# A pointwise convolution with folded depthwise weights on one core: splitting the weight load, moving the first input load to ScalarE's queue, and reordering the last waits

## The chip, the core and the metric

The kernel runs on one core of one Trainium2 chip. The metric is the time of one execution on the device in microseconds (us). Every time below that is given from "the start of the span" comes from the profile of one execution. The profiled span is a little shorter than the timed execution: the span of the kernel before is 572.9 us, and the profiled execution itself was timed at 574.59 us.

The engines are called by their short names in the profile: PE is TensorE (its weight loads, which overlap its matmuls, have a row of their own, PEld), DVE is VectorE, ACT is ScalarE, POOL is GpSimd and SP is SyncE. A "q" behind a name (SPq, ACTq) means the engine's sequencer, for instance when it issues a DMA.

## The reference, cut to what matters

A depthwise convolution with a 1x1 window multiplies each channel by one number; a pointwise convolution then mixes the channels with a 384x384 matrix.

```python
H = W = 384; C = 384; k = 1          # x: (1, 384, 384, 384) bf16, dw: (1, 1, 384), pw: (384, 384)
xp = jnp.pad(x, ((0,0),(pad,pad),(pad,pad),(0,0)))         # pad = 0 for k = 1
out = jnp.zeros_like(x)
for i in range(k):
    for j in range(k):
        out = out + xp[:, i:i+H, j:j+W, :] * dw[i, j][None, None, None, :]
return jnp.einsum('bhwc,cd->bhwd', out, pw)
```

With a 1x1 window this is `x @ (diag(dw) @ pw)` for 147,456 pixels. x and the output have 113 MB each.

## The kernel before

The kernel scales `pw` by `dw` once, at the start, and then does one matrix product. The pixels are cut into 288 "supertiles" of 512. Each supertile is transposed by DVE (pairs of bf16 moved as 32-bit words, two instructions for the two halves of the channels), multiplied on PE in 48 matmuls, copied from PSUM to SBUF by ACT, and stored. Loads and stores handle 1 to 10 supertiles at a time ("chunks"); the first chunks have 1, 1, 2, 2 and 4 supertiles, and their loads are called x0 to x4 here. The loads go into three big buffers in rotation.

The start of the program prepares the folded weights `w_r`. Four things play a role there.

The loads, in the order of their issue (SP issues all but `dw`):

```python
nc.scalar.dma_start(dw_row[:], dw.rearrange("a e c -> a (e c)")).then_inc(s_dw, 16)
nc.sync.dma_start(pw_n[:], pw.rearrange("(k p) d -> p k d", p=P)).then_inc(s_pw, 16)
load_x(0)
# ... cut: SP goes on with x1, x2, x3, x4, then the loop of loads and stores
```

The small matmuls on PE. `idle_work(n)` issues 4n matmuls on constants ("fillers") whose result nobody reads; they keep PE occupied. The three matmuls on `dw_row` turn the row of depthwise weights into columns. Then 18 matmuls multiply `pw` by selection matrices `sel_w` that carry the depthwise weights; the table `times` says which of them are repeated for the sake of being busy:

```python
idle_work(4)
nc.tensor.wait_ge(s_dw, 16)
# ... cut: 3 matmuls on dw_row, then_inc(s_df)
idle_work(4)
nc.tensor.wait_ge(s_pw, 16)
times = {(1, 1): 3, (2, 0): 2}
for k in range(3):
    nc.tensor.wait_ge(s_sw, k + 1)
    for r in range(2):
        if k == 2:
            nc.tensor.wait_ge(*w_done[r])      # the PSUM half is free again: copy r is done
        for v in [0, 1] * times.get((k, r), 1):
            mm = nc.tensor.matmul(PS[(k + 1) % 2][:, 2 * r + v, :D],
                lhsT=sel_w[...k, r...], rhs=pw_n[64 * v : 64 * v + 64, k, :], ...)   # cut
        mm.then_inc(s_w)
```

The copies of the six weight parts out of PSUM. Part 1 is copied by DVE, the parts 0, 2, 3, 4 and 5 by ACT, in this order, each as soon as its matmuls are done. The first matmul of the main loop needs parts 0, 1, 2 and 3 and the first half of the first transposed supertile:

```python
w_eng = [1, 0, 1, 1, 1, 1]                                  # 0: DVE, 1: ACT
w_first = {(0, 0): [(0, 1), (1, 3)], (4, 0): [(1, 4)], (4, 1): [(1, 5)]}
```

DVE's own program in this stage is: the selection matrices (`sel`, `dw_f`, three `sel_w`), the copy of part 1, and then the transposes of supertiles 0, 1, 2 and so on, each after its load:

```python
if h == 0 and j == 0:
    nc.vector.wait_ge(sem, n)                               # this chunk's load
ins = nc.vector.transpose(out=Tw[:, 3 * h : 3 * h + 3], in_=Xw[...])     # cut
if jj >= 2:
    ins._wait_ge(s_pe, 2 * (jj - 2) + h + 1)                # the buffer is free again
ins.then_inc(s_t[s][h])
```

At the end, the last supertile is copied by ACT and DVE together, in four pieces, and stored in two parts, and SP waits for the last stores:

```python
if jj + 1 == NS:
    nc.vector.wait_ge(s_o[g % NR], 16 * sum(map(len, groups[g % NR : g : NR])))
    nc.vector.wait_ge(s_pe, 2 * jj + 2)
    nc.scalar.wait_ge(s_pe, 2 * jj + 2)
    for q in (0, 2):
        nc.scalar.copy(Ov[:, q, j, :], PS[s][:, q, :D]).then_inc(s_a[s])
        nc.vector.tensor_copy(Ov[:, q + 1, j, :], PS[s][:, q + 1, :D]).then_inc(s_d)
    continue
```

```python
for o in sorted(range(NR), key=lambda o: (o - len(groups)) % NR):      # the order 2, 0, 1
    n = sum(n_parts[t] for t, c in enumerate(chunks) if c[0] % NR == o)
    nc.sync.wait_ge(s_o[o], 16 * n)
```

Of the kernel before, what the change touches and what calls it, by code (L numbers as in the profile page):

```python
# [13 lines left out]
NR = 3  # L14
# [4 lines left out]
def _groups(n_super: int):  # L19

    head, tail = [[1, 1, 2, 2, 4]], [[6, 4], [4, 2, 1, 1]]
    mid = n_super - sum(map(sum, head + tail))
    assert mid > 0 and mid % LMAX == 0
    return head + [[LMAX]] * (mid // LMAX) + tail
# [3 lines left out]
def kernel(  # L28
# [12 lines left out]
    nc = tc.nc  # L41
    P = nc.NUM_PARTITIONS
    B, H, W, C = x.shape
# [10 lines left out]
    groups = _groups(NS)  # L54
# [14 lines left out]
    pw_n = consts.tile([P, 3, D], BF16, name="pw_n")  # L69
# [19 lines left out]
    s_pe = nc.alloc_semaphore("s_pe")  # L89
# [2 lines left out]
    s_o = [nc.alloc_semaphore(f"s_o{i}") for i in range(NR)]  # L92
    s_dw = nc.alloc_semaphore("s_dw")
    s_pw = nc.alloc_semaphore("s_pw")
    s_df = nc.alloc_semaphore("s_df")
    s_sw = nc.alloc_semaphore("s_sw")
    s_dwf = nc.alloc_semaphore("s_dwf")
# [4 lines left out]
    with tc.tile_critical(sync_engine=mybir.EngineType.Pool, no_gpsimd_drain=True):  # L102
        def x_of(t):
            g, i, off, first, L = chunks[t]
            n = first + LONG - NS
            if n >= 0:
                return Xl[:, 4 * n : 4 * n + 4, :], s_xl[n], 16
            n = sum(len(ls) > i for ls in groups[g % NR : g + 1 : NR])
            return Xs[g % NR][:, 4 * off : 4 * (off + L), :], s_x[g % NR][i], 16 * n

        def load_x(t, eng=nc.sync):
            g, i, off, first, L = chunks[t]
            dst, sem, _ = x_of(t)
            rows = xf[512 * first : 512 * (first + L), :]
            if first + LONG < NS:
                src = rows.rearrange("(p s) c -> p (s c)", p=P)
                dst = dst.rearrange("p s c -> p (s c)")
                if i == 0 and g >= NR:
                    je = g_end[g - NR]
                    eng.wait_ge(s_t[je % 2][1], je // 2 + 1)  # L120
            else:
                src = rows.rearrange("(a k q) c -> q a k c", k=4, q=4)
            eng.dma_start(dst, src).then_inc(sem, 16)
# [22 lines left out]


        nc.scalar.dma_start(dw_row[:], dw.rearrange("a e c -> a (e c)")).then_inc(s_dw, 16)
        nc.sync.dma_start(pw_n[:], pw.rearrange("(k p) d -> p k d", p=P)).then_inc(s_pw, 16)
        load_x(0)  # L150

        todo = []
        for t, (g, i, off, first, L) in enumerate(chunks):
# [4 lines left out]
        for _, f, a in sorted(todo, key=lambda a: a[0]):  # L158
# [4 lines left out]
                for _ in range(28):  # L163
                    nc.sync.wait_ge(s_pw, 16)
            f(*a)
        for o in sorted(range(NR), key=lambda o: (o - len(groups)) % NR):
            n = sum(n_parts[t] for t, c in enumerate(chunks) if c[0] % NR == o)
            nc.sync.wait_ge(s_o[o], 16 * n)

# [37 lines left out]
        def idle_work(n):  # L207
            for _ in range(n):
                for i in range(4):
                    nc.tensor.matmul(  # L210
                        PS[0][:, 2 * (i % 2) + i // 2, :D],
                        lhsT=ones[32 * i : 32 * i + 32, 0:P],
                        rhs=ones[32 * i : 32 * i + 32, :],
                        start=True,
                        stop=True,
                        tile_position=(32 * i, 0),
                    )
# [10 lines left out]
                stop=True,  # L228
            )
        mm.then_inc(s_df)  # L230
        idle_work(4)
        nc.tensor.wait_ge(s_pw, 16)
        times = {(1, 1): 3, (2, 0): 2}
        for k in range(3):
            nc.tensor.wait_ge(s_sw, k + 1)
            for r in range(2):
                if k == 2:
                    nc.tensor.wait_ge(*w_done[r])

                for v in [0, 1] * times.get((k, r), 1):  # L240
                    mm = nc.tensor.matmul(  # L241
                        PS[(k + 1) % 2][:, 2 * r + v, :D],
                        lhsT=sel_w[64 * v : 64 * v + 64, k, r, :, :].rearrange("p q w -> p (q w)"),
                        rhs=pw_n[64 * v : 64 * v + 64, k, :],
                        start=True,
                        stop=True,
                        tile_position=(64 * v, 0),
                    )
                mm.then_inc(s_w)
# [18 lines left out]
        def transposes(t, j):  # L268
            g, i, off, first, L = chunks[t]
            jj = first + j  # L270
            s = jj % 2
            X, sem, n = x_of(t)
            Xw = X.bitcast(U32).rearrange("p (k l) c -> p k l c", l=L)
            Tw = Ts[s][:].bitcast(U32).rearrange("p b (i k) -> p b k i", k=4)
            for h in range(2):
                if h == 0 and j == 0:
                    nc.vector.wait_ge(sem, n)
                ins = nc.vector.transpose(  # L278
                    out=Tw[:, 3 * h : 3 * h + 3],
                    in_=Xw[:, :, j, 96 * h : 96 * h + 96].rearrange("p k (b w) -> p b k w", w=32),  # L280
                )
                if jj >= 2:
                    ins._wait_ge(s_pe, 2 * (jj - 2) + h + 1)
                ins.then_inc(s_t[s][h])
# [29 lines left out]
        for jj, (t, j) in enumerate(order):  # L314
            g, i, off, first, L = chunks[t]
            s = jj % 2
            Ov = Os[g % NR][:, 4 * off * D : 4 * (off + L) * D].rearrange("p (q j d) -> p q j d", q=4, d=D)
            if j == 0 and i == 0 and g >= NR:
                nc.scalar.wait_ge(s_o[g % NR], 16 * sum(map(len, groups[g % NR : g : NR])))
            if jj + 1 == NS:  # L320
                nc.vector.wait_ge(s_o[g % NR], 16 * sum(map(len, groups[g % NR : g : NR])))
                nc.vector.wait_ge(s_pe, 2 * jj + 2)
                nc.scalar.wait_ge(s_pe, 2 * jj + 2)
                for q in (0, 2):
                    nc.scalar.copy(Ov[:, q, j, :], PS[s][:, q, :D]).then_inc(s_a[s])  # L325
                    nc.vector.tensor_copy(Ov[:, q + 1, j, :], PS[s][:, q + 1, :D]).then_inc(s_d)  # L326
                continue
            a = nc.scalar.copy(Ov[:, :, j, :], PS[s][:, :, :D])  # L328
            a._wait_ge(s_pe, 2 * jj + 2)
            a.then_inc(s_a[s])  # L330

            if jj in LONG_AT:
                load_x(NT - LONG + LONG_AT.index(jj), nc.scalar)
            if jj + 2 < NS:
                transposes(*order[jj + 2])
# [30 lines left out]
```

## Time and profile before

| what | value |
|---|---|
| time, median of 3 runs | 574.9 us (574.84 to 575.03) |
| profiled span | 572.9 us |
| busy PE matmul / PEld / DVE / ACT | 566.9 / 412.3 / 508.0 / 418.7 us |
| moved over DMA, mean rate | 226.88 MB, 396 GB/s |
| main-loop matmuls | 13,824, busy 561.8 us |
| first main-loop matmul starts at | 6.76 us |
| landing after issue: pw, x0, x1, x2 | 2.9, 3.3, 5.6, 7.0 us |

The table is read from the start of the page (busy times, DMA), from its list of the costliest groups (the matmuls), from the timeline (the start of the main loop) and from the DMA view with a window on one issue at a time (the landings). 561.8 us of matmuls in 288 supertiles are 1.95 us for each. What lies outside of the main loop is 6.76 us at the start and the few microseconds from the last matmul to the end of the span.

### The profile page before, as it was taken

Reading aid. Unit: us, or ns where it says so; the run is one execution under the profiler, and the core shown is the slowest. Engines: PE = TensorE matmul, PEld = TensorE weight load, DVE = VectorE, ACT = ScalarE, POOL = GpSimd, SP = SyncE. Lnnn points to the kernel's source line nnn. Section 1 sums busy time; section 2 is a strip of 40 time slices with the busy share of each in tenths; the row PEclk is TensorE's granted clock in tenths of the full one; section 3 lists DMA queues with packets and bytes.
Section 4 is the critical chain, followed back from the end, with each engine's and each line's share of the span. In section 5 each row is a group of like instructions: output and inputs, shape, how many; then the busy total and the mean of one; then the engine's idle time right before and its main releaser. Section 6 shows DMA issues by size and latency. Waiting matters only on the chain.

```text
span 572.9 us, 29723 instructions
## 1 busy us (share of the span) xinstructions
PE 566.9 (99%) x13877; PEld 412.3 (72%) x13877; DVE 508.0 (89%) x584; ACT 418.7 (73%) x297; POOL 0.5 (0%) x5
## 2 busy tenths in 40 slices
PE   8999999999999999999999999999999999999996
PEld 5777777777777777777777777777777777777774
DVE  7899999999999999999999999999999999999995
ACT  6777777777777777777777777777777777777775
POOL 0000000000000000000000000000000000000000
PEclk9999999999999999999999999999999999999999
DMA  8999999999999999999999999999999999999676
GB/s 323 435 374 428 424 419 433 433 431 417 431 404 424 390 403 409 418 390 393 437 391 391 400 425 398 389 414 428 398 385 428 405 389 401 422 398 373 262 285 245
DMA packets 26453, 226.88 MB, mean 396 GB/s; under 512 B 1226, under 2 KB 6987, under 8 KB 22603
## 3 DMA queue, kind: packets, MB, share of 16 engines
q1 hardware_dynamic: 25408, 226.01, 97.3%
q10 hardware_dynamic: 1034, 0.79, 0.4%
q14 instruction: 10, 0.07, 0.0%
q8 instruction: 1, 0.02, 0.0%
HBM read 113.54 MB, written 113.25 MB: 396 GB/s over the span
## 4 chain that ended last, share of the span: by engine, by line
PE 98%; ACT 1%; DMA 0%; DVE 0%; issue 0%; DVEq 0%
PE ps L193 97%; PE ps L210 0%; DMA out_dram<-O 0%; ACT w_r L291 0%; ACT O L328 0%; DVE O L326 0%; DVEq L102 0%; PE ps L241 0%; PE ps L223 0%
## 5 line engine op out<-in xcount | busy, mean ns | idle before, releaser
L193 PE MATMUL ps<-w_r,T 32*128 32x384 bf16 x13824 | 561.8, 321 | 0.5 <-ACT w_r L291 0.5
L278 DVE STREAM_TRANSPOSE T<-X 128x384 uint32<-128x384 uint32 x572 | 501.2, 881 | 54.9 <-DMA X<-in_x_dram 2.9
L328 ACT CAST O<-ps 128x1536 bf16<-128x1536 f32 x287 | 412.7, 1438 | 147.3 <-PE ps L193 147.3
L193 PEld LDWEIGHTS ps<-w_r,T 32*128 32x128 bf16 x13824 | 410.0, 93 | 152.3 <-issue 0.9
L291 ACT CAST w_r<-ps 128x768 bf16<-128x768 f32 x5 | 3.6, 820 | 1.3 <-PE ps L241 1.3
L210 PE MATMUL ps<-const-bfloat16-1.0 32*128 32x384 bf16 x32 | 2.8, 517 | 1.1 <-PEq L350 1.1
L278 DVE STREAM_TRANSPOSE T<-Xl 128x384 uint32<-128x384 uint32 x4 | 3.5, 880 | 0.4
L326 DVE CAST O<-ps 128x384 bf16<-128x384 f32 x2 | 1.0, 552 | 3.1 <-DMA out_dram<-O 3.1
L266 ACT ACT_TABLE_LOAD x1 | 1.3, 1283 | 1.5 <-POOLq L102 1.5
L241 PE MATMUL ps<-pw_n,sel_w 64*128 64x384 bf16 x18 | 2.4, 423 | 0.0
L210 PEld LDWEIGHTS ps<-const-bfloat16-1.0 32*128 32x128 bf16 x32 | 1.1, 124 | 1.6 <-issue 1.4
L241 PEld LDWEIGHTS ps<-pw_n,sel_w 64*128 64x128 bf16 x18 | 1.0, 120 | 1.6 <-issue 0.7
L291 DVE CAST w_r<-ps 128x768 bf16<-128x768 f32 x1 | 1.0, 959 | 1.0 <-PE ps L241 1.0
L296 DVE TENSOR_REDUCE sel<-eye 128x64 f32<-128x128 bf16 x1 | 0.3, 289 | 1.5 <-POOL eye L256 1.5
L325 ACT CAST O<-ps 128x384 bf16<-128x384 f32 x2 | 0.9, 482 | 0.5 <-PE ps L193 0.5
L303 DVE COPY dw_f<-ps 128x3 f32<-128x3 f32 x1 | 0.2, 160 | 0.9 <-PE ps L223 0.9
L306 DVE TENSOR_SCALAR sel_w<-sel,dw_f 128x256 bf16<-128x256 f32 x3 | 0.9, 349 | 0.0
L223 PEld LDWEIGHTS ps<-const-bfloat16-1.0,dw_row 1*128 1x128 bf16 x3 | 0.3, 115 | 0.4 <-DMA dw_row<-in_dw_dram 0.4
L256 POOL TENSOR_SCALAR_AFFINE_SELECT eye<-const-bfloat16-1.0 128x128 bf16<-128x128 bf16 x1 | 0.3, 292 | 0.6 <-POOLq L102 0.6
L266 ACT COPY warm<-const-float32-0.0 128x1 f32<-128x1 f32 x2 | 0.3, 188 | 0.0
L223 PE MATMUL ps<-const-bfloat16-1.0,dw_row 1*128 1x1 bf16 x3 | 0.3, 176 | 0.0
L350 POOL MEMSET const-bfloat16-1.0<- 128x1 bf16 x1 | 0.1, 102 | 0.0
(3 smaller groups left out, 0.3 us busy)
## 6 DMA issues: line engine op xcount, KB each, us to landing
X<-in_x_dram SPq DMA_DIRECT2D x26, 3840.0 KB, 21.9
out_dram<-O SPq DMA_DIRECT2D x26, 3840.0 KB, 27.7
X<-in_x_dram SPq DMA_DIRECT2D x3, 1536.0 KB, 17.9
out_dram<-O SPq DMA_DIRECT2D x4, 768.0 KB, 9.3
out_dram<-O SPq DMA_DIRECT2D x2, 1536.0 KB, 15.1
X<-in_x_dram SPq DMA_DIRECT2D x3, 768.0 KB, 8.4
X<-in_x_dram SPq DMA_DIRECT2D x1, 2304.0 KB, 19.6
out_dram<-O SPq DMA_DIRECT2D x1, 2304.0 KB, 11.4
```

Of the source, the lines that this page charges most:

```text
L193: mm = nc.tensor.matmul(PS[s][:, q, :D], lhsT=Ts[s][32 * q : 32 * q + 32, b, par::2], rhs=w_r[32 * q : 32 * q + 32, b, par, :], start=(b, ...
L210: nc.tensor.matmul(PS[0][:, 2 * (i % 2) + i // 2, :D], lhsT=ones[32 * i : 32 * i + 32, 0:P], rhs=ones[32 * i : 32 * i + 32, :], start=True ...
L223: mm = nc.tensor.matmul(PS[1][:, 0, D + k : D + k + 1], lhsT=dw_row[:, P * k : P * k + P], rhs=ones[0:1, 0:1], start=True, stop=True,)
L241: mm = nc.tensor.matmul(PS[(k + 1) % 2][:, 2 * r + v, :D], lhsT=sel_w[64 * v : 64 * v + 64, k, r, :, :].rearrange("p q w -> p (q w)"), rhs ...
L256: nc.gpsimd.affine_select(out=eye[:], in_=ones[:, 0:P], pattern=[[-1, P]], compare_op=mybir.AluOpType.is_equal, fill=0.0, base=0, channel_ ...
L266: nc.scalar.copy(warm[:, s : s + 1], nc.const_aps.tensor(0.0, [P, 1], F32)).then_inc(s_a[s])
L278: ins = nc.vector.transpose(out=Tw[:, 3 * h : 3 * h + 3], in_=Xw[:, :, j, 96 * h : 96 * h + 96].rearrange("p k (b w) -> p b k w", w=32),)
L291: o = nc.vector.tensor_copy(out, in_) if e == 0 else nc.scalar.copy(out, in_)
L306: nc.vector.tensor_scalar_mul(sel_w[:, k], sel[:].unsqueeze(2).to_broadcast([P, 2, 4, 32]), dw_f[:, k : k + 1]).then_inc(s_sw)
L325: nc.scalar.copy(Ov[:, q, j, :], PS[s][:, q, :D]).then_inc(s_a[s])
L326: nc.vector.tensor_copy(Ov[:, q + 1, j, :], PS[s][:, q + 1, :D]).then_inc(s_d)
L328: a = nc.scalar.copy(Ov[:, :, j, :], PS[s][:, :, :D])
```

## The change

The change touches the start and the end of the program; the main loop is the same.

1. `pw`'s first 128 rows, which the first four of the weight matmuls need, are loaded by a DMA of their own with their own semaphore (96 KB); the other 256 rows follow in a second DMA (192 KB). It is meant to let the weight matmuls of `k = 0` begin before all of `pw` is there.
2. The first input load, x0, is issued by ScalarE, so that SP has again as many issues ahead of x1 as before.
3. The second group of fillers shrinks from 16 matmuls to 8, and the repeated weight matmuls move: three rounds for (1, 1) become one, and (2, 1) gets two. The weight stage has 16 matmuls in place of 18.
4. At the end, SP waits for the three store semaphores in the order 1, 0, 2 in place of 2, 0, 1, and DVE waits for PE ahead of the stores in the program text. In the built programs the wait that stands first in the text is the one that ends up on the instruction itself, and the others become semaphore instructions ahead of it. So in the program before, DVE's copy carries the wait for an old store and a separate instruction waits for PE; after the change the copy carries the wait for PE. Likewise SP's closing branch carried the wait for the buffer 2, and carries that for the buffer 1, which is stored last, after the change.

```diff
-        nc.sync.dma_start(pw_n[:], pw.rearrange("(k p) d -> p k d", p=P)).then_inc(s_pw, 16)
-        load_x(0)
+        nc.sync.dma_start(pw_n[:, 0], pw[0:P, :]).then_inc(s_pw, 16)
+        nc.sync.dma_start(pw_n[:, 1:3], pw[P:C, :].rearrange("(k p) d -> p k d", p=P)).then_inc(s_pw2, 16)
+        load_x(0, nc.scalar)
@@ SP's last waits
-        for o in sorted(range(NR), key=lambda o: (o - len(groups)) % NR):
+        for o in sorted(range(NR), key=lambda o: (len(groups) - 1 - o) % NR):
@@ PE's start
-        idle_work(4)
+        idle_work(2)
         nc.tensor.wait_ge(s_pw, 16)
-        times = {(1, 1): 3, (2, 0): 2}
+        times = {(2, 0): 2, (2, 1): 2}
         for k in range(3):
+            if k == 1:
+                nc.tensor.wait_ge(s_pw2, 16)
             nc.tensor.wait_ge(s_sw, k + 1)
@@ the last supertile
             if jj + 1 == NS:
+                nc.vector.wait_ge(s_pe, 2 * jj + 2)
                 nc.vector.wait_ge(s_o[g % NR], 16 * sum(map(len, groups[g % NR : g : NR])))
-                nc.vector.wait_ge(s_pe, 2 * jj + 2)
```

(Cut: the allocation of the semaphore `s_pw2`.)

More of the change, by code (lines that the diff above doesn't have):

```diff
@@ L94 @@
     s_pw = nc.alloc_semaphore("s_pw")
+    s_pw2 = nc.alloc_semaphore("s_pw2")
     s_df = nc.alloc_semaphore("s_df")
```

## The prediction

> **What bounds the kernel now.** I read the chain that ended last first, because a change at the two ends of a program can only be worth what those ends take from it. Its columns are start, length (both us) and what ran.
>
> ```profile
> 0.80 0.32 issue
> 1.12 1.49 PE ps L210 x16
> 2.61 0.03 PE ps L223
> 2.64 1.30 PE ps L210 x13
> 3.94 0.45 PE ps L241 x2
> 4.39 0.02 issue
> 4.41 2.21 ACT w_r L291 x3
> 6.62 0.14 issue
> 6.76 557.91 PE ps L193 x13728
> ```
>
> The last row is the main loop. It never stops: 288 supertiles of 1.95 us are 561.6 us, and 6.76 + 561.6 = 568.4, while the last supertile's copy starts at 568.59. So the time is the start (6.76), the loop (561.6) and what follows (572.9 - 568.4 = 4.5 us). No part of the change touches the middle term. Only the start and the end, 11.3 us together, are in play, and 2% would be 11.5 us.
>
> The chain puts the filler (L210) ahead of the first weight matmul at 3.94. That is not what released it. The timeline of 3.8 to 7.2 us (start, length, engine, line, operation, then the idle time before it and what ended it) says that it was the load of pw:
>
> ```profile
> 3.87 0.13 PEld L241 LDWEIGHTS ps<-pw_n,sel_w 64*128 64x128 bf16 x4 [0.62 <-DMA pw_n<-in_pw_dram]
> ...
> 4.41 3.61 ACT L291 CAST w_r<-ps 128x768 bf16<-128x768 f32 x5 [1.33 <-PE ps L241]
> ...
> 5.61 1.55 DVE L278 STREAM_TRANSPOSE T<-X 128x384 uint32<-128x384 uint32 x2
> ```
>
> So the start is a relay: pw lands at 0.96 + 2.9 = 3.82; PE makes part 0 (3.87 to about 4.4); ACT copies parts 0, 2, 3 (4.41 to 6.62), after which PE starts with 0.14 us of issue. The five copies take 3.61 us, their starts some 0.69 apart. The transposes of x0 start at 5.61 with no idle time before them: x0, landed at 1.45 + 3.3 = 4.8, had been waiting for DVE.
>
> Just behind it stand the next two loads. The same timeline from 7.2 to 11 us:
>
> ```profile
> 7.60 1.58 DVE L278 STREAM_TRANSPOSE T<-X 128x384 uint32<-128x384 uint32 x2 [0.45 <-DMA X<-in_x_dram]
> ```
>
> x1 landed at 1.97 + 5.6 = 7.58. DVE's first half of it takes 0.88 (mean on the page), to 8.48; with the 0.14 us that PE's issue took above, supertile 1 can start at 8.62, and it does start at 6.76 + 1.95 = 8.71. **Slack 0.09 us.** For x2: transposed from 9.56 (idle before it, ended by its DMA), 9.56 + 0.88 + 0.14 = 10.58 against 10.66, slack 0.08. So three things end almost together: the weights, x1 and x2.
>
> The end, in the timeline from 568.5 on:
>
> ```profile
> 568.59 0.86 ACT L325 CAST O<-ps 128x384 bf16<-128x384 f32 x2 [0.51 <-PE ps L193]
> 568.66 1.02 DVE L326 CAST O<-ps 128x384 bf16<-128x384 f32 x2 [3.08 <-DMA out_dram<-O]
> 569.24 0.85 SPq L142 DMA_DIRECT2D out_dram<-O  x2
> ```
>
> ACT and DVE wait for the same last matmul; DVE starts 0.07 later. "DMA out_dram" is named because that wait sits on the copy, but that store was long done.
>
> **What the Trainium skill says.** "DMA: Bandwidth & Descriptors", section "Queues, rings and completion order": SP and ACT each have a ring on each of the same 16 DMA engines, and an engine alternates between rings, but only after draining a whole packet of several descriptors. The trace before fits: a 384 KB load that ACT issues at 24.55 us begins to move only near 28.7 and lands near 43, because SP's ring is full of large transfers. [...] Here pw's last data packet starts at about 3.4 and the load counts as landed at 3.82: some 0.37 us after that packet's end, so splitting a load does not split this part. "TensorE: Matmul & The Clock Gate", Part 1, says that PE runs at half clock until a free-running window of about 3.4 us has been busy. In the trace, groups of weight matmuls start 0.32 us apart until about 5.1 and 0.16 apart from 5.4 on, some 4.3 us after PE's first filler at 1.12.
>
> **The change, part by part.**
>
> *pw's first rows.* The first 128 of pw's 384 packets had moved by about 2.7 us in the packet records; with the 0.37 for the receipt the small load lands near 3.1. The next wait takes over: `sel_w` for k = 0 is written by DVE from 2.87 to about 3.22, and PE has seen it at 3.3. So the first weight matmul starts near 3.37 in place of 3.87, and ACT's first copy near 3.91. With the copies unchanged (2.21 + 0.14) the loop could start at 6.26: **0.50 us at most**. The fillers are no obstacle: 8 of them, from 2.4 in groups of four 0.32 us apart, are through near 3.2.
>
> *pw's other rows.* Parts 2 and 3 need the second load. From its landing f the path is 0.05 + 0.50 (matmul) + 0.04 + 0.69 + 0.82 (two copies) + 0.14 = 2.24. The start is max(6.26, f + 2.24), break-even at f = 4.52. If pw's second part moves ahead of x0 on the engines, as today, f is about 3.85 and nothing is lost. If x0 on the other ring gets in between, its 8 packets of 0.12 us per engine come ahead of up to 16 of pw, about 1 us: f near 4.4 (finely mixed) to 4.8 (x0 first), so the start is 6.64 to 7.04.
>
> *x0 on ScalarE's queue.* SP issues about every 0.49 us. pw takes two slots now, so x1 keeps the third (1.97); x0 is issued by ACT behind dw at about 1.5, as early as before. The same 1.06 MB must move by x1's landing and the same 1.84 MB by x2's. I find nothing that brings x1 or x2 forward. In the packet records a few engines spend 1.0 to 1.8 us on their first packet of x1 (4.1 to 4.3 us) and of x2, which makes them late; nothing in the change addresses that. ACT's table load (1.28) and its two small copies move back by about 0.5, to end near 3.6, still ahead of 3.91.
>
> *Gain at the start, then:* the loop's end follows the latest of the three gates. If x1 and x2 land as before, supertiles 1 and 2 start 0.09 and 0.08 earlier at best, and the other 0.4 us becomes an idle gap of PE between supertiles 0 and 1. **About -0.08 us.**
>
> *The last waits.* DVE's copy starts with ACT's: -0.07 on the path, as its second copy (ends 569.68) releases the last store. SP's closing branch passes one semaphore instruction less after the last landing: in the records that instruction and the branch behind it start at 571.71 and 571.78, so -0.07. **About -0.13 us**, and this is the safest part.
>
> Sum: 574.9 - 0.08 - 0.13 = 574.7.
>
> **The rivals.** (1) *The full half microsecond arrives*: x1 and x2 land earlier as well, because two rings hide those long first packets or because x0 no longer stands ahead of them in SP's ring. Then -0.50 - 0.13 gives 574.3. For it: the DMA rate was only 164 to 292 GB/s between 4.4 and 6.8 us against 410 after that, so there is room. Against: bytes and issue times are the same. (2) *pw's second load becomes the wait*: x0 gets in front, f is 4.8, the loop starts at 7.04, +0.28 - 0.13 gives 575.05. For it: engines alternate between rings, and by 2.6 us some engines are still busy with pw's first rows, so x0 is next. Against: with pw's second part at 1.45 and x0 at about 1.5, pw's descriptors should be first on an idle engine. (3) *The clock*: with 8 fillers and 2 weight matmuls less, PE has more gaps before 5.4. If the switch to full clock slips past the start of the loop by 1 us, that microsecond yields half, +0.5. For it: idle from about 3.9 if f is late. Against: the first copies, not PE, set the pace, and the repeats in k = 2 fill the time from about 4.7 on.
>
> **Range and chances.** Roughly half of the weight goes to the small gain near 574.7, a sixth to rival 1, a third to rivals 2 and 3 with 575.0 to 575.3. The runs before spread over 0.2 us. Range 574.2 to 575.3. 2% is out of reach either way.
>
> **What would show it.** The first weight matmul at 3.3 to 3.5, released by DVE or the load; ACT's first copy near 3.9; the gap between its first and second copy (0.69 if f is early, over 1 us if rival 2 holds); the first L193 matmul at 6.2 to 6.7; a gap in PE before supertile 1 that a transpose of x1 ends; the spacing of weight matmuls for the clock; DVE's last copy level with ACT's. The prediction is wrong if x1 and x2 land half a microsecond or more away from 7.6 and 9.5 us, in either direction, or if the clock switches late.

## The result, and the profile after

| | before | after |
|---|---|---|
| time, median | 575.0 us (6 runs) | 576.84 us (6 runs, 576.24 to 577.43) |
| ratio, 95% interval | | 1.0028 (1.0015 to 1.0041) |
| profiled span | 572.87 us | 575.71 us |
| pw (after: its second part) lands | 3.82 us | 6.37 us |
| x0 lands | 4.78 us | 6.54 us |
| first main-loop matmul | 6.76 us | 8.44 us |
| first supertile on PE | 1.95 us | 3.26 us |
| ACT's first last copy to the end of the span | 4.28 us | 4.14 us |

The changed kernel is slower by 1.8 us, 0.3% of the time. The profiled execution is the slowest of the six (577.43 us), 2.84 us above that of the kernel before, so it shows more loss than the median does. Its account is exact for itself: the loop starts 1.68 us later, the first supertile takes 1.31 more, the end takes 0.14 less. The sum is +2.85; the spans differ by 2.84.

The chain that ended last, after the change (start, length, what):

```profile
1.40 4.98 DMA pw_n<-in_pw_dram
6.37 0.05 issue
6.42 0.35 PE ps L245 x2
6.77 0.02 issue
6.80 1.51 ACT w_r L295 x2
8.30 0.14 issue
8.44 559.21 PE ps L195 x13063
```

Before, this chain named PE's fillers and three copies by ACT. Now one DMA holds 4.98 us of it: the second part of pw, issued at 1.40. Behind it come only two copies, as the copy of part 0 was done long before. The timeline of the same stretch shows the two sides of the split (start, length, engine, line, operation, and the idle time before it):

```profile
3.37 0.82 PE L245 MATMUL ps<-pw_n,sel_w 64*128 64x384 bf16 x4
3.91 0.80 ACT L295 CAST w_r<-ps 128x768 bf16<-128x768 f32 x1 [0.40 <-PE ps L245]
...
6.42 1.15 PE L245 MATMUL ps<-pw_n,sel_w 64*128 64x384 bf16 x12 [2.23 <-DMA pw_n<-in_pw_dram]
6.57 2.93 DVE L282 STREAM_TRANSPOSE T<-X 128x384 uint32<-128x384 uint32 x4 [1.38 <-DMA X<-in_x_dram]
...
8.44 3.27 PE L195 MATMUL ps<-w_r,T 32*128 32x384 bf16 x44 [0.87 <-ACT w_r L295]
```

The first part did what it was meant to do: its matmuls start at 3.37, not 3.87. Then PE is idle for 2.23 us and waits for the second part, and x0 has become late as well (DVE idle for 1.38).

The last row shows a second loss: the 44 matmuls of the loop that are recorded up to the end of this view (11.5 us) take 3.27 us. The view by stretches of 2 us says why. Its columns are the stretch and its length, the busy time (and count) of PE, PEld, DVE, ACT and POOL, the clock granted to PE (1.00 is full), the busy share of the DMA engines, and GB/s:

```profile
6.00:8.00 2.00, 1.15 (x12) 0.50 (x12) 1.43 (x3) 1.20 (x2) 0.00 (x0) 0.93 1.01 412
8.00:10.00 2.00, 1.56 (x21) 0.90 (x25) 1.50 (x3) 1.70 (x3) 0.00 (x0) 0.50 1.07 449
10.00:12.00 2.00, 2.00 (x40) 1.28 (x36) 0.94 (x2) 0.08 (x1) 0.00 (x0) 0.72 1.02 436
```

The clock record itself has half clock from 7.73 to 11.14 us, one window of 3.41 us after a window (4.31 to 7.73) in which PE had idled for some 2 us. The loop thus ran at half clock from 8.44 to 11.14. That is 2.70 us for the work of 1.35, a loss of 1.35; the first supertile shows 1.31. Not every execution lost its clock in this way: the mean of the clock record is 0.996 in this one and one other, and 0.998 to 0.999 in the other four. The mean leaves out the time ahead of the first grant, so a late first grant, as in the swapped run below, would not show in it.

At the end, ACT and DVE now start together:

```profile
571.57 0.86 ACT L329 CAST O<-ps 128x384 bf16<-128x384 f32 x2 [0.51 <-PE ps L195]
571.58 1.02 DVE L330 CAST O<-ps 128x384 bf16<-128x384 f32 x2 [3.02 <-DMA out_dram<-O]
```

### The profile page after: what moved, and what is told of

The parts are those of the page before. It is cut to its first block, busy times and chain, and to the rows that moved or that the text cites. A ratio compares the mean times of both kernels' runs of the same rounds, so it can differ in the third digit from the quotient of the medians.

```text
span 575.7 us, 29705 instructions
## 1 busy us (share of the span) xinstructions
PE 567.2 (99%) x13867; PEld 386.3 (67%) x13867; DVE 507.0 (88%) x584; ACT 419.1 (73%) x297; POOL 0.5 (0%) x5
## 4 chain that ended last, share of the span: by engine, by line
PE 97%; DMA 1%; ACT 1%; issue 0%; DVE 0%; DVEq 0%; SPq 0%; POOLq 0%
PE ps L195 97%; DMA pw_n<-in_pw_dram 1%; DMA out_dram<-O 0%; ACT w_r L295 0%; ACT O L332 0%; DVE O L330 0%; DVEq L103 0%; SPq L150 0%; PE ps L245 0%; SPq L365 0%; POOLq L103 0%; POOLq L354 0%
## 5 line engine op out<-in xcount | busy, mean ns | idle before, releaser
L195 PEld LDWEIGHTS ps<-w_r,T 32*128 32x128 bf16 x13824 | 384.9, 93 | 179.1 <-issue 1.2
```

The costliest lines, as they stand in the source:

```text
L195: mm = nc.tensor.matmul(PS[s][:, q, :D], lhsT=Ts[s][32 * q : 32 * q + 32, b, par::2], rhs=w_r[32 * q : 32 * q + 32, b, par, :], start=(b, ...
```

## The experiments

The theory after reading the result, called A: x0 on ScalarE's ring and pw's second part on SP's are on the same 16 DMA engines at the same time, take turns, and delay each other; PE's idle time then costs the clock as well. Its rival, B: the split itself is at fault, a second DMA for pw being late on any ring. Ten runs of nine kernels were made in three groups, each group beside the kernel before (medians 574.95, 574.91 and 574.99 us); the ratios are to it. The changed kernel itself was not run again in these groups.

### x0 back on SP

```diff
-        load_x(0, nc.scalar)
+        load_x(0)
```

> The changed kernel with one thing undone: x0 is issued by SP again, behind both parts of pw. Theory A (x0 on ScalarE's ring takes turns with pw's second part on the same DMA engines, and that is what made that part land 5.0 us after its issue): on one ring the second part goes ahead of x0 and lands 2.3 to 2.7 us after its issue, near 3.9 us; the first main-loop matmul moves from 8.44 to 6.3 to 6.7 us, at full clock, and the time is 574.5 to 575.0. Theory B (the split itself costs: a second DMA for pw is late on any ring): the second part still lands after 5.5 us, the loop starts after 7.5 us and the time stays near 576.8.

Measured: 574.39 us, ratio 0.9993 (0.9984 to 1.0001). The chain that ended last:

```profile
1.40 2.96 DMA pw_n<-in_pw_dram
...
6.43 557.90 PE ps L195 x13728
```

With the split and everything else of the change in place, the second part lands 2.0 us earlier, the loop starts at 6.43, and 2.45 us of the time are gone. B falls. This is also the first version below both kernels, though the interval of its ratio to the kernel before reaches 1.

### x0 on ScalarE, pw in one piece

```diff
-        load_x(0)                       # kernel before
+        load_x(0, nc.scalar)
```

> The kernel before with one thing changed: x0 is issued by ScalarE; pw stays one load of 288 KB, fillers and last waits as before. Theory A: pw now shares the engines with x0 from its first third on and lands at 5 to 6.5 us in place of 3.8; the loop then starts 2.9 us after pw's landing, at 8 to 9.4 us, with the clock at half for a part of its first microseconds; time 576 to 578. Theory B: pw lands near 3.8 as before and the time stays at 574.9.

Measured: 574.96 us, ratio 1.0005 (0.9997 to 1.0014), no difference. Theory A in the form that I had put down fails here: pw landed at 3.96, not 5 to 6.5. It was x0 that paid, landing at 6.09 in place of 4.78, and it set the start at 7.09, as the timeline shows:

```profile
6.12 5.98 DVE L278 STREAM_TRANSPOSE T<-X 128x384 uint32<-128x384 uint32 x8 [0.29 <-DMA X<-in_x_dram]
7.09 4.73 PE L193 MATMUL ps<-w_r,T 32*128 32x384 bf16 x111 [0.30 <-DVE T L278]
```

The landings of all the profiles with these four arrangements, in us from the start of the span (those of the later experiments are included):

| pw (or its second part) / x0 lands | x0 on SP's ring | x0 on ScalarE's ring |
|---|---|---|
| pw in one load | 3.82 / 4.78, 4.01 / 4.97, 3.99 / 4.91 | 3.96 / 6.09 |
| pw in two loads | 4.36 / 5.31, 3.88 / 5.61, 4.05 / 5.93 | 6.37 / 6.54, 5.91 / 5.88, 5.82 / 5.97 |

Splitting alone moves pw's end by little more than it wanders, moving x0 alone does not move it, and both together move it by 1.8 us or more. Neither half of the change is the cause by itself. What both together do is to bring the issues of the two loads close to each other: pw's one load is issued at 0.95, x0 at 1.53, while pw's second part is issued at 1.40 and x0 at 1.52. Yet in both kernels half of pw's 384 packets have started when x0's first one moves (190 at 2.89 here, 189 at 2.82 in the changed kernel). By 3.25 it is 326 here and 252 there. Why pw's one load keeps ahead of x0 and its second part does not is not shown. This one profile also has hardly any of the slow packets that are counted below (one of x0's takes over 0.5 us, none of pw's).

### x0 on ScalarE, but later

```diff
+        nc.scalar.wait_ge(s_pw, 16)
         load_x(0, nc.scalar)
```

> The changed kernel with x0 still on ScalarE's ring, but issued only when pw's first part has landed (3.0 us in place of 1.5). Theory (the second part of pw is late because its descriptors and x0's come to the engines at the same time and are then served in turns): with x0 out of the way the second part lands at 3.9 to 4.5 us. x0 then lands near 6.5 and sets the start of the loop, some 1.05 us later, at 7.4 to 7.8 us. Rival (a ring of ScalarE in use slows SP's ring whenever): the second part still lands after 5.5 us.

Measured: 582.83 us (2 runs), ratio 1.0137 (1.0117 to 1.0157). The second part of pw landed at 3.91, 2.5 us after its issue: with x0 out of the way in time it is not late, on the same two rings. That is the point of this run, and it went as expected. What did not: x0, issued at 3.04, landed at 11.60, not near 6.5. In its packet records x0's first packet moves only at 6.72, and x0 lands last, behind the three loads that SP had issued before it (x1 at 5.42, x2 at 8.59, x3 at 11.42). The chain and two rows of the view by stretches:

```profile
3.04 8.55 DMA X<-in_x_dram
11.60 0.02 issue
11.62 0.87 DVE T L283
12.49 0.09 issue
12.58 560.42 PE ps L196 x13721
```

```profile
7.00:8.00 1.00, 0.00 (x0) 0.00 (x0) 0.00 (x0) 1.00 (x3) 0.00 (x0) 0.75 0.97 363
8.00:9.00 1.00, 0.00 (x0) 0.00 (x0) 0.00 (x0) 0.52 (x1) 0.00 (x0) 0.50 0.99 409
```

PE idles for nearly 6 us (from 6.7 to 12.58), and the clock (second row, 0.50) stays at half until 17.7 us: three windows in a row.

### The two loads swapped

```diff
-        nc.sync.dma_start(pw_n[:, 1:3], ...).then_inc(s_pw2, 16)
-        load_x(0, nc.scalar)
+        nc.scalar.dma_start(pw_n[:, 1:3], ...).then_inc(s_pw2, 16)
+        load_x(0)
```

> The changed kernel with the two loads swapped: pw's second part is issued by ScalarE, x0 by SP behind pw's first part. Theory (the rings take turns, whichever is whose): the second part is late again, landing at 5 to 6.4 us, the loop starts at 7.1 to 8.4 us and the time is 575.5 to 577. Rival (ScalarE's ring is served first): the second part lands near 4 us, x0 later than 5.5, and the time is near 575.

Measured: 576.6 us, ratio 1.0038 (1.0024 to 1.0052). The second part is late on ScalarE's ring too, landing at 5.50 (issue 1.53 + 4.0), and x0 lands at 5.20. So it isn't that one ring is served first. The timeline has the same two marks as the changed kernel, PE's idle time ahead of pw's second part and a long wait for the first supertile:

```profile
5.54 2.10 PE L245 MATMUL ps<-pw_n,sel_w 64*128 64x384 bf16 x12 [1.35 <-DMA pw_n<-in_pw_dram]
...
10.89 1.44 ACT L332 CAST O<-ps 128x1536 bf16<-128x1536 f32 x1 [1.90 <-PE ps L195]
```

The manner differs, though: here the second part's first packet moves only at 3.62, after most of x0's, and 214 of its 256 packets then move within half a microsecond. "In turns" describes the changed kernel, "one behind the other" this one. And the clock is lost in another way: full clock is granted for the first time at 9.77, 2.0 us after the start of the loop at 7.73.

### Fillers in the gap

```diff
             if k == 1:
+                idle_work(13)            # the next run: idle_work(6)
                 nc.tensor.wait_ge(s_pw2, 16)
```

> The changed kernel with 13 more groups of fillers (52 matmuls) ahead of the wait for pw's second part, so that PE isn't idle from 4.2 to 6.4 us. Theory A with the clock as a second term: pw's second part still lands near 6.4 and the loop still starts near 8.4, but the granted clock does not drop behind it, the first supertile takes 1.95 us in place of 3.26, and the time is 1.0 to 1.4 us under the changed kernel's, near 575.6. Rival (the slow first supertile is due to late inputs, not to the clock): the first supertile stays over 3 us and the time near 576.8.

Measured: 577.26 us, ratio 1.0035 (1.0024 to 1.0045); the miss was mine. The fillers ran at half clock (the switch came at 7.01 in this run) and lasted to 7.8 us, 1.9 past the landing of pw's second part at 5.91, so the loop started at 9.78. The first supertile did take 1.95 us, but the total says nothing. So with fewer:

> The changed kernel with 6 more groups of fillers ahead of the wait for pw's second part, few enough to end before that part lands (6 groups of 0.16 to 0.32 us from 4.2 on end by 6.1 us). Theory (the second term of the loss is the clock, which drops because PE idles from 4.2 to 6.4 us): the loop still starts near 8.4, the first supertiles take 1.95 us each in most runs, and the time is about 1 us under the changed kernel's, near 575.8. Rival (fillers don't matter; the second term is something else): 576.8.

Measured: 575.92 us, ratio 1.0015 (1.0008 to 1.0022), 0.9 us under the changed kernel. The two were measured in different groups and the intervals of their ratios touch, but the executions do not meet: 575.30 to 576.16 in 20 here, 576.24 to 577.43 in 6 there. The timeline, and the view by stretches at the start of the loop:

```profile
4.13 2.10 PE L212 MATMUL ps<-const-bfloat16-1.0 32*128 32x384 bf16 x24
...
6.16 1.77 PE L246 MATMUL ps<-pw_n,sel_w 64*128 64x384 bf16 x12
6.71 2.91 ACT L296 CAST w_r<-ps 128x768 bf16<-128x768 f32 x4 [2.00 <-PE ps L246]
8.35 3.43 PE L195 MATMUL ps<-w_r,T 32*128 32x384 bf16 x80 [0.41 <-ACT w_r L296]
```

```profile
8.00:10.00 2.00, 1.65 (x44) 1.26 (x47) 1.39 (x3) 1.61 (x3) 0.00 (x0) 1.00 1.08 452
```

PE has no gap ahead of the weight matmuls, the loop starts at 8.35, as late as in the changed kernel, and 80 matmuls are recorded in 3.43 us where there were 44 in 3.27. The granted clock is 1.00 where it was 0.50. The second term of the loss is the clock, and it follows from the first: 24 matmuls that compute nothing make the kernel faster. (pw's second part landed at 5.82 here, 0.55 earlier than in the profile of the changed kernel; the fillers ended 0.3 too late to use that.)

### Fewer fillers alone

```diff
-        idle_work(4)                     # the second group, kernel before
+        idle_work(2)
-        times = {(1, 1): 3, (2, 0): 2}
+        times = {(2, 0): 2, (2, 1): 2}
```

> The kernel before with the fewer fillers and the moved repeats alone; loads and last waits as before. Theory (fillers matter only where PE would idle long enough for the clock to drop): pw still lands near 3.9 and the loop starts at 6.7 to 7.0 us; PE is idle for some 0.5 us more ahead of pw, too short to move the clock's switch beyond the start of the loop, so the time is 574.8 to 575.1. Rival (8 fillers fewer are enough to lose the window): the first supertile takes over 2.5 us and the time is over 575.4.

Measured: 575.49 us, ratio 1.0012 (1.0003 to 1.002). The theory fails: 8 fillers fewer cost 0.5 us. In the profile the full clock is recorded only from 7.33, after the loop's start at 6.92, and the first supertile takes 2.14 us. That is half a proof: x1 landed late in this run as well (7.97), and its transpose ends at about the time at which PE goes on, and the moment of the switch to full clock wanders from one execution to the next (below). The profiled execution is also the fastest of the 13 (574.93), and half clock from 6.92 to 7.33 costs it only 0.2 us. So how the 0.5 of the median divides between the clock and x1 stays open.

### The split on one ring, with the old fillers

```diff
         # from: the changed kernel with x0 on SP
-        idle_work(2);  times = {(2, 0): 2, (2, 1): 2}
+        idle_work(4);  times = {(1, 1): 3, (2, 0): 2}
```

> The changed kernel with x0 on SP as in the first experiment, and with the 16 fillers and the repeats of the kernel before. Theory: the longer filler keeps PE busy until about 3.7, so the first weight matmul starts near 3.7 in place of 3.37; the second copy of ScalarE then starts near 4.9, the loop near 6.5, about 0.1 later than with 8 fillers: time 574.4 to 574.6. Rival (fewer fillers had nothing to do with it): the same start, near 6.4.

Measured: 574.63 us, ratio 0.9997 (0.9988 to 1.0005). The first weight matmul starts at 3.87, ACT's first copy at 4.29, its second at 4.99, the loop at 6.64, all 0.1 to 0.2 later than expected. The direction is as expected: the longer filler stands in the way once pw's first part is early. Fewer fillers, with the moved repeats, thus cost 0.5 us where pw is late and gain some 0.2 where it is early, the latter within the spread of the runs.

### The last waits alone

```diff
-        for o in sorted(range(NR), key=lambda o: (o - len(groups)) % NR):
+        for o in sorted(range(NR), key=lambda o: (len(groups) - 1 - o) % NR):
-                nc.vector.wait_ge(s_o[g % NR], ...)
                 nc.vector.wait_ge(s_pe, 2 * jj + 2)
+                nc.vector.wait_ge(s_o[g % NR], ...)
```

> The kernel before with the reordered last waits alone. Theory: DVE's first piece of the last supertile starts with ACT's in place of 0.07 us later, and SP's closing branch follows the last landing at once, so that the stretch from ACT's last copies to the end of the span is 4.13 us in place of 4.28; start and loop are unchanged; time 0.13 us under the kernel before. Rival (that stretch is set by the store's landing and the closing steps of the other engines): 4.28 and no difference.

Measured: 574.67 us, ratio 0.9997 (0.9989 to 1.0006). The total is too coarse to tell, but the profile isn't. ACT and DVE start within 0.01 of each other where they stood 0.07 apart, and the stretch from 568.78 to the end of the span takes 4.14 us, against 4.28 before:

```profile
568.78 0.86 ACT L325 CAST O<-ps 128x384 bf16<-128x384 f32 x2 [0.51 <-PE ps L193]
568.78 1.02 DVE L326 CAST O<-ps 128x384 bf16<-128x384 f32 x2 [3.01 <-DMA out_dram<-O]
```

Over the profiles of this study this stretch is 4.13 to 4.14 us in all nine with the new order, and 4.28 in the three with the old one. No other term here is so steady.

### The better version again

> The kernel of the first experiment (the changed kernel with x0 back on SP) once more, in more rounds, as the version that should beat both. Expected: second part of pw at 3.9 to 4.4 us, loop from 6.3 to 6.5 us, end stretch 4.14 us, time 574.3 to 574.5, ratio to the kernel before near 0.9991 with an interval below 1.

Measured: 574.4 us, ratio 0.9993 (0.9985 to 1.0001). The median repeats (574.39 and 574.40, some 0.6 under the kernel before), and both intervals just reach 1, so it is not more than probable that it beats the kernel before. It beats the changed kernel by 2.4 us. In this run's profile the loop starts at 6.92 although pw's second part landed at 4.05: x0 landed at 5.93 and set the start. So the landings move by half a microsecond from one execution to another, and which load ends the start changes with them.

## Why the prediction was wrong

I had 574.7 us with a range to 575.3; it is 576.84. By its own steps:

- **pw's first rows: right.** Landing 3.01 (near 3.1 predicted), first weight matmul 3.37 (3.37), ACT's first copy 3.91 (3.91), fillers no obstacle.
- **pw's other rows: this is the step that failed.** The main line let pw's second part move ahead of x0, with f at 3.85 and nothing lost; the second rival let x0 in between, with f at 4.4 to 4.8. f was 6.37 in the profile of the changed kernel, and 5.91 and 5.82 in the two kernels with the same loads. So the second rival had the mechanism, and its term was too small: x0 beside pw costs f 2.0 to 2.5 us, where I had 0.5 to 1. I had given x0's 8 packets per engine 0.12 us each. In the packet records of the changed kernel 10 of x0's 128 packets take 0.5 to 1.8 us; they start between 3.2 and 4.0 us, and the DMA rate is 154 GB/s in the half microsecond behind 4.0 and 231 in the next. In the other two profiles only 2 and none of x0's packets take 0.5 us or more, but 5 and 6 of pw's second part do (up to 1.2 us). With x0 behind pw on SP's ring there are such packets as well, but they fall on the loads behind: 6, 14 and 11 on x0 and x1 in the three profiles, and 1, 0 and 0 on pw. I had seen them in the trace before, on x1, and taken them for x1's own. What makes these packets slow no run here tells.
- **The path behind f: right.** f + 2.24 would give 8.61, the loop starts at 8.44; most of the 0.17 is that the weight matmuls ran at full clock (0.35 for two in place of 0.50).
- **x0 "as early as before": wrong.** It was issued at 1.52 as said, and landed at 6.54. An early issue on a second ring was not an early landing in any of the runs on ScalarE's ring with x0 at 1.52 (5.88 to 6.54).
- **The gates of x1 and x2: wrong as gates.** I had held that nothing could start the loop much before 6.67, since x1 and x2 would land as before. In the first experiment, where both are issued 0.4 us later than before, x1 landed at 6.38 and x2 at 8.82, and the loop ran without a gap from 6.43. In the three profiles of kernels with x1's issue at 1.97 behind x0 on SP it landed at 7.58, 7.18 and 7.97. One profile's landing is one draw; a slack of 0.09 us worked out from it is no bound. (Of the bytes, 1.84 MB by x2's landing should read 1.82; nothing hangs on it.)
- **The clock: right as a rival, wrong as an alternative.** I gave it and the late load a third of the weight together, +0.5 or +0.28. The late load brings the idle time that brings the clock: in the profiled execution 1.31 on top of 1.68, and about 0.9 between the medians with and without the fillers in the gap. The guess that the repeats in k = 2 fill PE's time failed because k = 2 comes behind the late load.
- **The last waits: right.** -0.13 predicted, 4.28 to 4.14 measured. One reading was not: "DMA out_dram" is named at DVE's wait after the change too (571.58), when the copy carries the wait for PE, so the name does not tell which wait sits on the copy.

That x0 beside pw's second part makes it late is shown by taking x0 away, behind pw on SP's ring or later on ScalarE's. What remains open is the share of each ingredient in the lateness: slow packets, turns between the rings, and the start behind loads issued before.

## What to carry to other kernels

Here a second queue was not a second path: two loads issued 0.1 us apart on different rings finished together and late (5.5 to 6.5 us), while one behind the other on one ring the urgent one finished first (3.9 to 4.4). Holding the second load back on its own ring freed the first one but made the second so late that the time rose by 8 us. So give the load on the path the first place, try the next one behind it on the same ring, and read from several profiles, not from one, how far the landings wander. And when a change can make TensorE wait in the warm-up, count the clock in the same sum as the wait: in the profile, PE idle for 2 us cost 1.3 us more afterwards, and a few matmuls that compute nothing bought about 0.9 back in the median.

## What the runs showed of the hardware

Single packets can alternate. The packet records do not name the DMA engine, but in the changed kernel one can be followed by its times: packets of pw (0.036 us each) start at 5.157, 5.308 and 5.459 us, and packets of x0 (0.121 us each) at 5.190, 5.341 and 5.492 between them. The page of the Trainium skill that the prediction leaned on ("DMA: Bandwidth & Descriptors", "Queues, rings and completion order") speaks of a whole packet of typically 9 to 17 descriptors before an engine switches. If a record here is one descriptor, these alternate one by one, and the measurement decides. It is no rule either: in the swapped run, between 4.0 and 4.5 us, 214 packets of pw start on ScalarE's ring and only 9 of input loads on SP's.

The start of full clock wanders, which fits the free-running window of the skill's page "TensorE: Matmul & The Clock Gate" (Part 1): in the nine profiles of kernels that had no long idle time of PE at the start, or had it filled, full clock is recorded from times between 4.0 and 7.5 us on. In the changed kernel it was granted at 4.3, only to be taken back at 7.73, one window of 3.41 us later. It does not take one long idle time: in the run with x0 later the clock granted at 4.08 was taken back at 7.49, and PE had no idle time longer than 1.34 us in between, but its matmuls were busy for only some 1.3 us of the 3.41.
